# A third score room for the first 34 tiles, q's blocks by DMA, and new durations in the planner of an attention and mixing kernel

## The chip, the core and the metric

The kernel runs on one core of a Trainium2 chip. A core has five engines that run side by side, each through its own list of instructions in order: TensorE (PE, with its weight loads PEld), VectorE (DVE), ScalarE (ACT), GpSimd (POOL) and SyncE (SP). SP starts DMA transfers here. An instruction waits on semaphores until what it needs is there, and everything behind it on the same engine waits with it. The metric is device time in microseconds (us) of one execution, less is better.

## The reference, cut to what matters

```python
# attention: batch 8, heads 8, seq 576, head_dim 64; q, k, v, tau float32
scores = q @ k.T / sqrt(64)
keep   = scores >= max(scores, axis=-1) - tau
attn   = exp(scores - max) where keep, else 0
attn   = attn / (sum(attn) + 1e-9)
x      = (attn @ v), heads side by side          # [8, 576, 512]
# mixing: d_model 512, a causal convolution of 5 taps along seq for each channel
gate_pre[s] = sum over k of conv_w[k] * x[s + k - 4]
out    = (sigmoid(gate_pre) * (x @ w_val)) @ w_out
```

The two weight matrices and `conv_w` come as float64 and are turned into float32 on the chip.

## The kernel before, in words

The work is cut into 32 *jobs*, one for each batch and pair of heads. A job has nine *score tiles* of 128 query rows against 576 keys: one tile that holds the left-over 64 rows of both heads (the *left-over tile*, made from `kh`, `kl` and the block-diagonal `bdq`), and four tiles for each head (from `KH`, `KL` and `Q`). A float32 factor is split into a high and a low part of type float32r, and their products are summed, hence the names that end in h and l.

The life of one tile, with the lines of the profile: TensorE multiplies it into a *score room* `s` of two PSUM banks (L482). DVE takes the row maximum (L486). ACT forms `e`, the exponential (L492), and the threshold (L494). DVE compares, multiplies and sums (L508), and with that the score room is free again. The sums are inverted (POOL L525, DVE L527), the tile is divided by POOL, DVE or ACT (L538, L536, L534), turned by TensorE into `tp` (L588) and copied by ACT into `T` (L599). When half a job's tiles are turned, TensorE multiplies `T` with `v` into a room `acc` of one bank (L627, L634, called *attending* here), and ACT copies it to `xT` (L642). For each job follow the split of `xT` (ACT L667, POOL L671), the first tap of the convolution on POOL (L676), four taps on DVE (L683) and the gate (L691). After the four jobs of a batch come its *products* on TensorE, 192 matmuls with `w_val` and `w_out` into `acc` (L725), with DVE (L752), ACT (L768, L789) and POOL (L772) between and behind them.

PSUM has eight banks: two score rooms (four banks), two rooms `tp`, and two rooms `acc`, which attending and products share.

The next job's k and q are fetched by SP (L304, L308). POOL scales q (L327), ACT and POOL split both (L312, L316, L320, L324), POOL places four blocks of 64 x 64 into `bdq` (L210, in `place`), and SP copies the parts into `KH`, `KL` and `Q` by DMA (L362, L381). While the first jobs run, the weights are turned from float64 as well: 16 pieces, each with five operations on DVE (L224 to L233), two on POOL (L236, L268) and two on ACT (L222, L265).

No loop sets the order. Each operation is declared with an engine, a due time, a planned cost (how long it holds the engine) and a planned time to its end; `carry_out` then runs through planned time, takes on each engine what can begin first, among those the one with the earliest due time, and emits it. So the planned durations and the number of rooms set the order of every engine. In the plan, POOL's operations and some of DVE's (class `DVEp`) exclude each other.

## Time and profile before

| | us |
|---|---|
| timed executions | 775.31, 775.84, 782.68 |
| median | 775.84 |
| span of the profiled execution | 776.5 |
| TensorE busy | 719.6 (93%) |
| VectorE busy | 644.3 (83%) |
| ScalarE busy | 647.2 (83%) |
| GpSimd busy | 475.7 (61%) |

The page gives the profiled execution by its span, from the first to the last instruction; it shows no other time of that execution. A share of busy time is an average over stages, so the stages have to be looked at one by one. TensorE's matmuls overlap one another and their ends are modelled: the mean length of one matmul is longer than the time it adds, and a TensorE that is shown busy is not always at its peak.

### The profile page before, as it was taken

Reading aid. Unit: us, or ns where it says so; the run is one execution under the profiler, and the core shown is the slowest. Engines: PE = TensorE matmul, PEld = TensorE weight load, DVE = VectorE, ACT = ScalarE, POOL = GpSimd, SP = SyncE. Lnnn points to the kernel's source line nnn. Section 1 sums busy time; section 2 is a strip of 40 time slices with the busy share of each in tenths; the row PEclk is TensorE's granted clock in tenths of the full one; section 3 lists DMA queues with packets and bytes.
Section 4 is the critical chain, followed back from the end, with each engine's and each line's share of the span. In section 5 each row is a group of like instructions: output and inputs, shape, how many; then the busy total and the mean of one; then the engine's idle time right before and its main releaser. Section 6 shows DMA issues by size and latency. Waiting matters only on the chain.

```text
span 776.5 us, 15682 instructions
## 1 busy us (share of the span) xinstructions
PE 719.6 (93%) x5216; PEld 607.0 (78%) x5216; DVE 644.3 (83%) x1359; ACT 647.2 (83%) x1477; POOL 475.7 (61%) x698
## 2 busy tenths in 40 slices
PE   3788778979999999999999999998999999999997
PEld 3556457867878888888888888887888888978897
DVE  5989998988888887999878887887888888899830
ACT  5898978978998889899889988897898989888832
POOL 4777655847676775677557675765556764745321
PEclk9999989999999999999999999999999999999999
DMA  6666553535464555555465565553555556540001
GB/s 183 172 170 153 151 149 86 151 91 151 124 156 118 125 148 146 141 135 138 111 164 118 129 152 142 143 131 79 152 151 123 126 136 163 144 98 26 32 31 62
DMA packets 51888, 99.03 MB, mean 128 GB/s; under 512 B 9056, under 2 KB 9056, under 8 KB 51808
## 3 DMA queue, kind: packets, MB, share of 16 engines
q1 hardware_dynamic: 51488, 97.47, 49.0%
q8 instruction: 42, 0.69, 0.4%
q10 hardware_dynamic: 320, 0.56, 0.3%
q14 instruction: 38, 0.31, 0.1%
HBM read 35.74 MB, written 9.44 MB: 58 GB/s over the span
## 4 chain that ended last, share of the span: by engine, by line
PE 68%; DVE 15%; DMA 5%; POOL 4%; ACT 4%; issue 2%; SPq 0%; POOLq 0%; ACTq 0%
PE acc L725 20%; PE s L482 17%; PE acc L634 14%; PE tp L588 13%; DVE nm L486 4%; DVE pp L508 4%; PE acc L627 3%; DMA q_r<-qT 3%; DVE pre L683 3%; ACT e L492 1%; POOL pp L538 1%; DVE spare L229 1%; DVE spare_m L231 1%; POOL ql L324 1%; DVE pp L536 1%
## 5 line engine op out<-in xcount | busy, mean ns | idle before, releaser
L486 DVE TENSOR_REDUCE nm<-s 128x1 f32<-128x576 f32 x288 | 214.9, 752 | 46.9 <-PE s L482 43.6
L492 ACT ACTIVATE e<-s,nm 128x576 f32<-128x576 f32 x288 | 215.3, 747 | 29.9 <-DVE nm L486 16.3
L508 DVE SCALAR_TENSOR_TENSOR pp<-s,nm,e 128x576 f32<-128x576 f32 x256 | 206.8, 811 | 19.9 <-ACT nm L494 18.3
L599 ACT COPY T<-tp 128x384 f32<-128x384 f32 x384 | 175.2, 488 | 26.3 <-PE tp L588 24.8
L482 PE MATMUL s<-KH,Q 128*128 128x288 f32 x512 | 163.4, 334 | 34.2 <-DVE pp L508 23.1
L588 PE MATMUL tp<-ident,pp 128*128 128x128 f32 x1152 | 183.3, 280 | 10.8 <-ACT pp L534 3.6
L588 PEld LDWEIGHTS tp<-ident,pp 128*128 128x128 f32 x1152 | 141.2, 143 | 20.9 <-ACT T L599 5.2
L482 PE MATMUL s<-KL,Q 128*128 128x288 f32 x512 | 147.0, 301 | 0.0
L482 PEld LDWEIGHTS s<-KH,Q 128*128 128x128 f32 x512 | 99.9, 195 | 59.6 <-DVE pp L508 32.2
L634 PE MATMUL acc<-T,v 128*64 128x256 f32 (+1 forms) x1024 | 141.2, 419 | 0.0
L538 POOL TENSOR_SCALAR pp<-pp,sums 128x576 f32<-128x576 f32 x124 | 106.9, 867 | 36.1 <-DVE sums L527 32.2
L683 DVE SCALAR_TENSOR_TENSOR pre<-xT,cw,pre 128x576 f32<-128x576 f32 x128 | 118.6, 926 | 8.8 <-POOL pre L676 8.7
L634 PEld LDWEIGHTS acc<-T,v 128*64 128x64 f32 x1024 | 69.1, 139 | 64.9 <-issue 28.0
L482 PEld LDWEIGHTS s<-KL,Q 128*128 128x128 f32 x512 | 99.9, 195 | 0.0
L525 POOL TENSOR_SCALAR sums<-sums 128x2 f32<-128x2 f32 (+1 forms) x160 | 46.9, 293 | 82.5 <-DVE pp L508 66.1
L494 ACT ACTIVATE nm<-nm,less 128x1 f32<-128x1 f32 x288 | 84.8, 294 | 0.0
L725 PE MATMUL acc<-xl,wvh 128*128 128x320 f32 (+1 forms) x256 | 78.3, 306 | 1.0 <-POOL xl L671 1.0
L725 PE MATMUL acc<-xh,wvl 128*128 128x320 f32 (+1 forms) x256 | 79.2, 309 | 0.0
L725 PE MATMUL acc<-gl,woh 128*128 128x320 f32 (+1 forms) x256 | 78.2, 305 | 1.1 <-POOL gl L772 1.1
L725 PE MATMUL acc<-xh,wvh 128*128 128x320 f32 (+1 forms) x256 | 78.6, 307 | 0.1
L725 PE MATMUL acc<-gh,wol 128*128 128x320 f32 (+1 forms) x256 | 78.6, 307 | 0.0
L725 PE MATMUL acc<-gh,woh 128*128 128x320 f32 (+1 forms) x256 | 78.4, 306 | 0.0
(81 smaller groups left out, 1279.8 us busy)
## 6 DMA issues: line engine op xcount, KB each, us to landing
KH<-kh SPq DMA_DIRECT2D x124, 144.0 KB, 2.6
KL<-kl SPq DMA_DIRECT2D x124, 144.0 KB, 3.5
k_r<-kT SPq DMA_DIRECT2D x32, 320.0 KB, 3.8
v<-vs SPq DMA_DIRECT2D x32, 320.0 KB, 2.9
q_r<-qT SPq DMA_DIRECT2D x32, 288.0 KB, 3.9
outT<-o SPq DMA_DIRECT2D x32, 288.0 KB, 2.4
Q<-qh SPq DMA_DIRECT2D x62, 128.0 KB, 2.3
Q<-ql SPq DMA_DIRECT2D x62, 128.0 KB, 2.4
```

What stands on the lines that cost most here:

```text
L482: nc.tensor.matmul(s[:, a, :HS], w, m, start=i == 0, stop=i == len(terms) - 1)
L486: nc.vector.tensor_reduce(self.nm[:, 0:1], self.s[:, :, :HS], axis=AX.XY, op=ALU.max, negate=True)
L492: nc.scalar.activation(self.e, self.s[:, :, :HS], AF.Exp, bias=self.nm[:, 0:1])
L494: nc.scalar.activation(self.nm[:, 1:2], self.nm[:, 0:1], AF.Identity, bias=less, scale=-1.0)
L508: nc.vector.scalar_tensor_tensor(grp.p[:, i * S : (i + 1) * S].rearrange("p (a f) -> p a f", a=2), self.s[:, :, :HS], self.nm[:, 1:2], self.e,
L525: add = op("POOL", k - 4, 0.2, 0.33, lambda: nc.gpsimd.tensor_scalar(sums(), sums(), 1.0, 1e-9, op0=ALU.mult, op1=ALU.add), [self.kept])
L538: nc.gpsimd.tensor_scalar(v, v, ri(i), 0.0, op0=ALU.mult, op1=ALU.add)
L588: nc.tensor.transpose(tp[:, i * P : (i + 1) * P], self.p[:, k0 : k0 + P], ident)
L599: nc.scalar.copy(T[:, c0 : c0 + n, self.off : self.off + P], tp[:, 0 : n * P].rearrange("p (c q) -> p c q", q=P),)
L634: nc.tensor.matmul(acc[hs, :w], t.v[:, c0 : c0 + D], T[:, h * NKC + c, :], start=False, stop=c == NKC - 1, skip_group_check=True,)
L683: nc.vector.scalar_tensor_tensor(cv, t.xT[:, i : i + S], cw[:, g, i : i + 1], cv, op0=ALU.mult, op1=ALU.add)
L725: nc.tensor.matmul(taken[name, e, j][:, :w], wt[:, c, c0 : c0 + P], moving(c, i)[:, hs], start=n == 0, stop=n == NM - 1,)
```

## The change

It has four parts.

- **Rooms.** `ps_3`, a pool of its own with one more score room (`third`, two banks), stands where the two `acc` banks were. Tiles take it in turn with the other two. When it is given back after tile 34 has been taken, the pool is closed, and its two banks become the two rooms `acc`. Until tile 34, attending uses the rooms `tp`. Products can begin only when `acc` exists.
- **q's blocks.** The four 64 x 64 blocks of each job are copied into `bdq` by SP with DMA, not by POOL.
- **Smaller pieces.** POOL's subtractions for `kl`, `ql`, `xl` and `gl` are cut in two by columns (320 + 320 or 320 + 256), and a product's matmul waits for its own half alone.
- **Planned durations.** An issue of a DMA is planned with 0.56 us (before 0.1, or 0.15 for a pair), landings and several other operations a little longer, and the addition to the sums is due 0.9 tiles earlier.

`Job`, `convolve` and `products` are also written so that a job could cover one half only; here every job has both halves, and this changes nothing by itself.

```diff
+    early = ExitStack()
+    ps_3 = early.enter_context(tc.tile_pool(name="ps_3", bufs=1, space=bass.MemoryType.PSUM))
...
+    class ScoreRooms(Rooms):
+        def __init__(self, pool, n, shape, dtype, name):
+            super().__init__(pool, n, shape, dtype, name)
+            self.third = ps_3.tile(shape, dtype, name="third")
+            self.free.append((0.0, self.third))
+            self.taken = 0
...
+        def give(self, room, when):
+            if room is self.third and self.taken >= THIRD_UNTIL:
+                early.close()
+                ps_a = ctx.enter_context(
+                    tc.tile_pool(name="ps_a", bufs=1, space=bass.MemoryType.PSUM)
+                )
+                for i in range(2):
+                    r_acc.give(ps_a.tile([P, 512], F32, name=f"acc{i}"), when)
+            else:
+                super().give(room, when)
...
-    r_acc = Rooms(ps_a, 2, [P, 512], F32, "acc")
+    r_acc = Rooms(None, 0, [P, 512], F32, "acc")
+    r_s = ScoreRooms(ps_s, 2, [P, 2, 512], F32, "s")
...
+    SEND = 0.56
+    def act(n):
+        return 0.1 + 0.00083 * n
+    def pool1(n):
+        return 0.13 + 0.00102 * n
+    def pool2(n):
+        return 0.17 + 0.00212 * n
+    def tapped(n):
+        return 0.068 + 0.00114 * n
...
-            got_q = op("SP", due - 6, 0.1, 3.8, fetch_q, takes=[r_qr])
+            got_q = op("SP", due - 6, SEND, 4.2, fetch_q, takes=[r_qr])
...
-            self.low_k = op("POOL", due + 1, 1.52, 1.62, low_k, [self.high_k], [r_kl],
-                            [(r_kr, lambda: self.k_r)])
+            for x in (0, SK // 2):
+                self.low_k = [op(
+                    "POOL", due + 1, pool2(SK // 2), pool2(SK // 2) + 0.1, low_k(x, x + SK // 2),
+                    self.low_k, [] if x else [r_kl], [(r_kr, lambda: self.k_r)] if x else [],
+                )]
...
-                        spread(self.bd[hs, which, hs], src[hs, 0:SL].bitcast(F32))
+                        nc.sync.dma_start(
+                            self.bd[hs, which, hs].bitcast(F32), src[hs, 0:SL].bitcast(F32)
+                        )
...
-            self.blocks = [op("POOL", due + 3, 0.45, 0.6, place(0), [high], [r_bd])]
-            self.blocks.append(op("POOL", due + 3, 0.45, 0.6, place(1), [low, self.blocks[0]]))
+            if 0 in self.js:
+                self.blocks = [op("SP", due + 3, 2 * SEND, 2.9, place(0), [high], [r_bd])]
+                self.blocks.append(op("SP", due + 3, 2 * SEND, 2.9, place(1), [low, self.blocks[0]]))
...
-                o = op("SP", due + 1, 0.15, 2.9, copies(name, rooms, src, 0), [done], [rooms])
+                o = op("SP", due + 1, 2 * SEND + 0.1, 3.7, copies(name, rooms, src, 0), done, [rooms])
...
-            add = op("POOL", k - 4, 0.2, 0.33, lambda: nc.gpsimd.tensor_scalar(
+            add = op("POOL", k - 4.9, 0.28, 0.38, lambda: nc.gpsimd.tensor_scalar(
...
-            others = {"DVEp": (0.375, 0.47), "ACT": (0.6, 0.72)}
+            others = {"DVEp": (0.43, 0.52), "ACT": (0.66, 0.78)}
...
+            rooms = r_tp if k < THIRD_UNTIL else r_acc
...
-            cost = 5 * w / 600 + 0.19
+            cost = 5 * w / 600 + 0.27
...
-                    after = [need[c][i], weights[name, c, c0 // CW * CW], *last]
+                    after = [*need[c][j][i], weights[name, c, c0 // CW * CW], *last]
```

What the planner makes of it is seen in the lists of the engines. First TensorE at the start of the program, from the second score tile on. `s0` and `s1` are the score rooms, `KH0` and `Q0` the first job's parts, `tp` the rooms of the transposes and `bdq0` the block-diagonal q; one matmul of each tile stands for its four. Before:

```order
L482 MATMUL s1_102<-KH0_117,Q0_115 128x288
...
L482 MATMUL s0_101<-KH0_117,Q0_115 128x288
...
L482 MATMUL s1_102<-KH0_117,Q0_115 128x288
...
L588 MATMUL tp0_103<-ident_96,pp2_131 128x128 x3
L588 MATMUL tp1_104<-ident_96,pp2_131 128x128 x3
L482 MATMUL s0_101<-kh0_109,bdq0_121 128x288 x2
```

And with the change:

```order
L556 MATMUL s1_104<-KH0_116,Q0_114 128x288
...
L556 MATMUL third_105<-KH0_116,Q0_114 128x288
...
L556 MATMUL s0_103<-KH0_116,Q0_114 128x288
...
L656 MATMUL tp0_101<-ident_96,pp2_130 128x128 x3
L656 MATMUL tp1_102<-ident_96,pp2_130 128x128 x3
L656 MATMUL tp0_101<-ident_96,pp2_130 128x128 x3
L656 MATMUL tp1_102<-ident_96,pp0_128 128x128 x3
L556 MATMUL s1_104<-kh0_108,bdq0_120 128x288 x2
```

The third tile goes into `third`, so it no longer waits until the first tile's room is free. In all, 11 of the 288 tiles go there.

Next SP in the middle of the program, from the copies of one job's Q to those of the next. `KH1`, `KL1` and `Q1` are one job's copies, `k_r0` and `q_r0` the raw k and q of the job after it, `v` its values. Before:

```order
L381 DMA Q1_116<-qh0_111 64x512 x2
L381 DMA Q1_116<-ql0_112 64x512 x2
L362 DMA KH1_118<-kh0_109 64x576 x2
L362 DMA KL1_120<-kl0_110 64x576 x2
L304 DMA k_r0_107<-kT 128x640
L362 DMA KH1_118<-kh0_109 64x576 x2
L362 DMA KL1_120<-kl0_110 64x576 x2
L308 DMA q_r0_108<-qT 128x576
L290 DMA v1_114<-vs 128x640
L381 DMA Q0_115<-qh0_111 64x512 x2
```

And with the change:

```order
L461 DMA Q1_115<-qh0_110 64x512 x2
L461 DMA Q1_115<-ql0_111 64x512 x2
L440 DMA KH1_117<-kh0_108 64x576 x2
L418 DMA bdq0_120<-qh0_110 64x64 x2
L440 DMA KH1_117<-kh0_108 64x576 x2
L440 DMA KL1_119<-kl0_109 64x576 x2
L354 DMA k_r0_106<-kT 128x640
L358 DMA q_r0_107<-qT 128x576
L418 DMA bdq0_120<-ql0_111 64x64 x2
L440 DMA KL1_119<-kl0_109 64x576 x2
L339 DMA v1_113<-vs 128x640
L461 DMA Q0_114<-qh0_110 64x512 x2
```

Two pairs of small DMAs for the next job's blocks now stand among the copies, and the fetch of q stands ahead of the last pair of copies and no longer behind it.

Last, POOL at the end of the program, the low parts `gl` of the last batch. Before:

```order
L671 TENSOR_TENSOR xl1_149<-xT1_141,xh1_143 128x576
L772 TENSOR_TENSOR gl0_162<-g0_156,gh0_158 128x576
L772 TENSOR_TENSOR gl1_163<-g1_157,gh1_159 128x576
L772 TENSOR_TENSOR gl2_164<-g0_156,gh2_160 128x576
L772 TENSOR_TENSOR gl3_165<-g1_157,gh3_161 128x576
```

And with the change:

```order
L862 TENSOR_TENSOR gl1_162<-g1_156,gh1_158 128x320
L862 TENSOR_TENSOR gl1_162<-g1_156,gh1_158 128x256
L862 TENSOR_TENSOR gl2_163<-g0_155,gh2_159 128x320
L862 TENSOR_TENSOR gl2_163<-g0_155,gh2_159 128x256
L862 TENSOR_TENSOR gl3_164<-g1_156,gh3_160 128x320
L862 TENSOR_TENSOR gl3_164<-g1_156,gh3_160 128x256
```

Each low part is two operations, and the first matmuls of the last products need the first of them alone.

## Rows read from the trace of the kernel before

**Rows 1.** The page: busy us of each engine, share of the span, instructions.

```profile
PE 719.6 (93%) x5216; PEld 607.0 (78%) x5216; DVE 644.3 (83%) x1359; ACT 647.2 (83%) x1477; POOL 475.7 (61%) x698
```

**Rows 2.** Busy us by stretch: length, PE, PEld, DVE, ACT, POOL, clock, DMA, GB/s.

```profile
8.00:100.00 92.00, 69.81 (x416) 52.43 (x417) 81.81 (x188) 78.05 (x181) 63.34 (x103) 0.96 0.63 168
100.00:181.00 81.00, 69.27 (x444) 54.74 (x445) 73.77 (x154) 63.88 (x146) 52.16 (x73) 0.89 0.43 112
181.00:500.00 319.00, 314.95 (x2377) 270.38 (x2374) 274.67 (x577) 285.26 (x654) 213.65 (x310) 1.00 0.56 141
500.00:550.00 50.00, 46.35 (x338) 39.36 (x338) 40.62 (x84) 41.54 (x95) 29.96 (x47) 0.97 0.46 113
550.00:743.00 193.00, 190.36 (x1437) 162.34 (x1435) 163.76 (x344) 166.44 (x383) 107.42 (x151) 1.00 0.43 110
```

**Rows 3.** Waits from 8 to 100 us: who waited for whom, total, times, longest.

```profile
DVE nm L486 <- PE s L482: 6.2, 13, 1.4
...
DVE pp L508 <- ACT nm L494: 2.4, 6, 0.7
```

**Rows 4.** Waits from 100 to 181 us.

```profile
DVE nm L486 <- PE s L482: 6.2, 7, 2.6
...
PE acc L627 <- DVE g L752: 2.9, 1, 2.9
```

**Rows 5.** Groups of DVE from 8 to 181 us: count, busy us, mean ns.

```profile
L486 DVE TENSOR_REDUCE nm<-s 128x1 f32<-128x576 f32 x62 | 46.2, 752 | 13.0 <-PE s L482 12.4
...
L683 DVE SCALAR_TENSOR_TENSOR pre<-xT,cw,pre 128x576 f32<-128x576 f32 x20 | 17.4, 872 | 0.0
L231 DVE TENSOR_SCALAR spare_m<-spare 128x256 int32<-128x256 int32 x16 | 10.1, 633 | 0.0
...
L229 DVE SCALAR_TENSOR_TENSOR spare<-woh,spare 128x256 f32<-128x256 f32 x8 | 8.3, 1039 | 0.0
```

**Rows 6.** Single lines over the whole span: shortest, median, longest ns.

```profile
L683 DVE SCALAR_TENSOR_TENSOR pre<-xT,cw,pre x128: 791/811/2090, 53.0 to 749.7; 128x576 f32<-128x576 f32 x128
...
L231 DVE TENSOR_SCALAR spare_m<-spare x16: 276/310/1632, 28.4 to 178.5; 128x256 int32<-128x256 int32 x16
...
L229 DVE SCALAR_TENSOR_TENSOR spare<-woh,spare x8: 414/1122/1637, 100.9 to 177.4; 128x256 f32<-128x256 f32 x8
```

**Rows 7.** Groups of POOL over the whole span.

```profile
L316 POOL TENSOR_TENSOR kl<-k_r,kh 128x640 fp32r<-128x640 f32 x32 | 51.2, 1600 | 14.3 <-ACT kh L312 13.3
...
L772 POOL TENSOR_TENSOR gl<-g,gh 128x576 fp32r<-128x576 f32 x32 | 46.8, 1464 | 19.9 <-ACT gh L768 19.3
...
L210 POOL TENSOR_SCALAR bdq<-ql 64x64 fp32r<-64x64 f32 x64 | 16.6, 259 | 3.8
```

**Rows 8.** SP from 500 to 550 us in order of time: start, us.

```profile
516.25 1.62 SPq L362 DMA_DIRECT2D KH<-kh  x2
517.92 1.23 SPq L362 DMA_DIRECT2D KL<-kl  x2
519.25 0.54 SPq L308 DMA_DIRECT2D q_r<-qT  x1
```

**Rows 9.** The chain that ended last, in the same stretch: start, us.

```profile
519.25 4.54 DMA q_r<-qT
...
525.87 2.62 DVE pp L536 x2
```

**Rows 10.** The copies of Q by SP: issue ns, and us from issue to landing.

```profile
L381 SPq DMA_DIRECT2D Q<-qh x62: 461/467/1259, 24.8 to 689.0; - x62
...
DMA to landing us min/median/max: 2.2/2.4/4.9
```

**Rows 11.** Waits from 740 to 777 us.

```profile
PE acc L725 <- POOL gl L772: 1.1, 1, 1.1
```

**Rows 12.** The tile bdq from 280 to 400 us: ns, first and last start.

```profile
L482 PE MATMUL s<-kh,bdq x20: 290/295/398, 295.2 to 382.0; 128*128 128x288 f32 x20
L210 POOL TENSOR_SCALAR bdq<-ql x12: 234/240/243, 280.1 to 387.5; 64x64 fp32r<-64x64 f32 x12
```

More of the change, by code (lines that the diff above doesn't have):

```diff
@@ L19 @@
 P = 128
-AHEAD = False
-TH = "ACT"
 DIVIDE = ("DVEp", "ACT")
@@ new lines, in low_q, with run @@
+            def low_q(x, y):
+                def run():
+                    if x == a:
+                        self.ql = r_ql.take()
+                    nc.gpsimd.tensor_sub(
+                        self.ql[:, x:y], self.q_r[:, x:y], self.qh[:, x:y].bitcast(F32)
+                    )
+                return run
+            def scale_q():
+                q = self.q_r[:, a:z]
+                nc.gpsimd.tensor_scalar(q, q, sc, 0.0, op0=ALU.mult, op1=ALU.add)
+            got_k = op("SP", due - 6, SEND, 4.2, fetch_k, takes=[r_kr])
@@ L338, in place @@
+            high = op("ACT", due + 1, act(w), act(w) + 0.18, high_q, [scaled], [r_qh])
+            cuts = [a, z] if len(self.js) == 1 else [a, HALVES[0].stop, z]
+            low = [high]
+            for x, y in zip(cuts, cuts[1:]):
+                low = [op(
+                    "POOL", due + 2, pool2(y - x), pool2(y - x) + 0.1, low_q(x, y), low,
+                    [r_ql] if x == a else [], [(r_qr, lambda: self.q_r)] if y == z else [],
+                )]
+            low = low[0]
             def place(which):
@@ L689, in gate, with products @@
         def gate():
-            cv = batch.pre[:, g, :]
+            cv = batch.pre[:, g, a:z]
             nc.scalar.activation(cv, cv, AF.Tanh, scale=0.5)
-        first = op("ACT", k, 0.565, 0.76, high, [t.got_x], [r_xh])
-        part_ = op("POOL", k + 1, 1.4, 1.5, low, [first], [r_xl])
-        last = op("POOL", k, 0.73, 0.8, tap0, [t.got_x, conv_ready, *batch.started],
-                  [r_pre] if g == 0 else [])
-        if g == 0:
+        first = op("ACT", k, act(n), act(n) + 0.19, high, [pair.got_x], [r_xh] if a == 0 else [])
+        last = op("POOL", k, pool1(n), pool1(n) + 0.08, tap0, [pair.got_x, conv_ready, *batch.started],
+                  [r_pre] if g == 0 and a == 0 else [])
+        lows, done = [], [first]
+        for j in js:
+            c = HALVES[j]
+            m = c.stop - c.start
+            done = [op("POOL", k + 1, pool2(m), pool2(m) + 0.1, low(c), done, [] if j else [r_xl])]
+            lows += done
+            batch.made[g][j] = ([first], done)
+        if g == 0 and a == 0:
             batch.started = [last]
         for i in range(1, KT):
-            last = op("DVEp", k + 0.6 * i, 0.74, 0.85, tap(i), [last])
-        free = op("SP", k, 0.0, 0.0, lambda: None, [last, part_], gives=[(r_xT, lambda: t.xT)])
-        batch.made[g] = [first, part_]
-        batch.gate[g] = op("ACT", k + 3, 0.59, 0.76, gate, [last])
-    def products(batch, k, last):
+            last = op("DVEp", k + 0.6 * i, tapped(n), tapped(n) + 0.11, tap(i), [last])
+        if z == S:
+            op("SP", k, 0.0, 0.0, lambda: None, [last, *lows], gives=[(r_xT, lambda: pair.xT)])
+        made = op("ACT", k + 3, act(n), act(n) + 0.17, gate, [last])
+        for j in js:
+            batch.gate[g][j] = made
+    def products(batch, k, last, js):
         b = batch.b
+        a, z = HALVES[js[0]].start, HALVES[js[-1]].stop
+        n_all = z - a
         gs, g, o = {}, {}, {}
@@ L829, in tile_thresholded_attention_gated_mix @@
     batches = [Batch(b) for b in range(B)]
-    for b in range(B):
-        for g in range(NP):
-            if b or g:
-                jobs.append(Job(len(jobs), b, g, len(jobs) * TILES))
+    at = 0
+    for b, g, js in units:
+        if at:
+            jobs.append(Job(len(jobs), pairs[b, g], js, at))
+        at += sum(5 if j == 0 else 4 for j in js)
     tiles = []
@@ L836, in tile_thresholded_attention_gated_mix @@
     for t in jobs:
-        batch = batches[t.b]
-        if t.g == 0:
-            batch.started = []
-        for j in range(2):
+        batch = batches[t.pair.b]
+        for j in t.js:
             half = Half(t, j)
@@ L852, in tile_thresholded_attention_gated_mix @@
             half.attended(len(tiles) - 1)
-        convolve(t, batch, len(tiles))
-        if t.g == NP - 1:
-            last = products(batch, len(tiles) + 4.0, last)
+        convolve(t.pair, batch, len(tiles), t.js)
+        if t.pair.g == NP - 1:
+            last = products(batch, len(tiles) + 4.0, last, t.js)
     carry_out()
```

221 lines of the change are left out of this document (122 added, 99 removed).

## Prediction, made before the change was run

> **What bounds the kernel now.** I read the page's busy times first, then the stretches, and then, in each stretch, the wait that ends last. The page has TensorE at 719.6 of 776.5 us [rows 1], which by itself says neither where the rest is lost nor that TensorE is the bound everywhere. The stretches say it [rows 2]. From 181 to 743 us TensorE is busy for 314.95 + 46.35 + 190.36 = 551.7 of 562 us; it lacks 10.3 us, 3.65 of them between 500 and 550. There TensorE is the bound, and DVE has room (274.67 of 319 in the first of the three). From 8 to 181 us it is the other way round: TensorE is busy for 69.81 + 69.27 = 139.1 of 173 us, and DVE for 81.81 + 73.77 = 155.6. DVE carries the softmax of every tile and the turning of the weights besides, and by 181 us it has reduced 62 tiles [rows 5]. The order of TensorE, of before and of the change, has behind the 63rd tile the same work left: both have attended six jobs there and issued 120 of the 1536 matmuls of products. So the time is about (when the 63rd tile is reached) + (a rest that TensorE fills to 98%), and what the change can win lies mostly in the first term.
>
> DVE's 17.4 us of idle time in that first stretch have two causes. It waits for scores: 6.2 us up to 100 us, with 2.4 more for the threshold from ACT [rows 3], and 6.2 us from 100 to 181 [rows 4]. The scores are late since TensorE waits for a room that DVE itself has to free, two rooms being all there are. Further, DVE is busy longer than it need be. The last multiplication that turns a piece of `w_out` takes 1039 ns in the mean [rows 5] and 414 at the least [rows 6]: 8 x 0.625 = 5.0 us. The mask takes 633 against 276: 16 x 0.357 = 5.7 us. The taps take 872 against 791: 20 x 0.081 = 1.6 us. Together 12.3 us. The longest tap lasts 2090 ns, 1.3 us over the shortest, which is near the length of one of POOL's subtractions (1.46 to 1.60 us) [rows 7].
>
> **The change, part by part.** *Third room.* While it exists, DVE can have three tiles' scores before it, and the idle time it can remove is that up to 100 us, 6.2 + 2.4 = 8.6 us [rows 3]. Ends: 0, if e's two buffers hold the tiles up instead, and 8.6. I take half, 4.3, because only 11 of the first 34 tiles use the room and ACT, at 78.05 of 92 us [rows 2], is not far from full either. What then comes late next is ACT's exponential. Attending in `tp` costs TensorE nothing that it does not have: it is idle a quarter of that stretch.
>
> *From tile 34 to tile 63* there are two score rooms again, and the idle time of 7.2 us (81 - 73.77) [rows 2] can go only through a better order: 2.9 us of TensorE's waiting there was attending that stood behind the products' room [rows 4]. Ends: 3 worse (a stop of that size of its own) and 6 better; I take 1.0 better.
>
> *Smaller pieces.* Each subtraction of 1.46 to 1.60 us [rows 7] becomes two of about half. From the rows of kl, (1600 ns for 640 columns) and gl (1464 for 576) about 2.1 ns a column remain, so the second start adds some 0.1 to 0.2 us: POOL's 128 subtractions grow by 13 to 26 us in all, and the blocks that leave POOL, 128 of 259 ns [rows 7], give back 33 us. POOL is busy for 115.5 of 173 us in the first stretch and covers both. The path gets what DVE waits less behind POOL: between 0 and half of the 12.3 us. I take 2.5, nearer to 0, since half of POOL's work in this stretch, the divisions and the weights' subtractions, is not cut.
>
> The Trainium skill (SBUF — State Buffer, section "SBUF: two separate sides") says that VectorE and GpSimd share a pair of ports by an exclusive lock, held for the whole instruction, so that the loser waits until the other ends. The trace agrees as far as the 2090 ns of a tap go. By that rule alone, with every wait behind a halved subtraction halved, the sum would be 3.7 us lower.
>
> *More divisions on DVE.* Up to tile 72 its order has 10 instead of 7, and two of the 16 pieces of weights come later than before. Priced by the cheapest near neighbour, a tap's 0.79 us [rows 6], three divisions are at most 2.4 us of DVE time, mostly behind 181 us, where DVE has room. I charge 0.5.
>
> *Planned durations, in the stretch from 181 us on.* In SP's list of before, q's fetch stands behind the copies; each pair of them holds SP for 1.2 to 1.6 us [rows 8] where the plan has 0.15. In one such place q_r was sent at 519.25 us and took 4.54 us, divisions came late, two of DVE took 2.62 us, and TensorE stood [rows 9]. The change plans 0.56 us for an issue and puts the fetch ahead of the last copies. Of the 10.3 us I take 2.0 back; ends: 7 better, and 4 worse if the new order has stops of its own.
>
> *Blocks by DMA.* This adds 128 issues to SP of about 0.47 us, 60 us over the span, and each pair lands some 2.4 us after its issue [rows 10], where POOL needed about 0.5 us for a pair. I cost it at nothing: between 280 and 400 us the first blocks were written at 280.1, and the first left-over tile to use any ran at 295.2 [rows 12], so at least 15 us cover 3 us more. Without that cover it costs 0.47 x 2 + 2.4 - 0.5 = 2.8 us a job.
>
> *The end.* TensorE waited 1.1 us for the last low part [rows 11]; with 320 of 576 columns it is ready about 0.65 us sooner (1.46 x 256/576) [rows 7]. I take 0.5.
>
> **Sum.** 4.3 + 1.0 + 2.5 - 0.5 + 2.0 + 0.5 = 9.8 us better: 776.5 - 9.8 = 766.7 us of span. The median of the runs is 0.66 below that span, so **766.0**. About 1% (7.8 us, to 768.1 or 783.6) is what a measurement of this kernel can tell from no change.
>
> **The rivals.**
>
> *No change to speak of.* DVE in the first stretch is bound by its own work, the third room only moves its waits to ACT's e, and the rest is as full as before. For it: DVE is at 90% there and ACT at 82%, and a list written ahead never fills an engine wholly. Against: the waits for scores are there in the rows. What is left is the end and a little of the order: 776.5 - 0.5 - 1 = 775, less 0.66: 774.
>
> *Slower: SP holds up the left-over tile.* The place is the pair of small DMAs between the two halves of `KH`. SP goes in order: when ACT's high part of q is late, SP stands, and both the copies behind it and the blocks reach TensorE late, which goes in order as well. The price is 2.8 us a job, as above. It decides from (9.8 + 7.8)/2.8, about six of the 31 jobs, on; with ten it gives 766 + 28 = 794, with eight 788. Against: the 15 us of cover. For: SP gets 60 us of issues more, and the rows of before know no block by DMA, of 256 bytes a row. On such rows the Trainium skill (DMA: Bandwidth & Descriptors, section "Specifications") says that transfers under 512 bytes lose the full rate, since they are read, changed and written back. No run here shows it yet; by it the landing would be late, and I let the longest landing seen, 4.9 us [rows 10], stand for that in the rows: 5.3 us a job, still within 15.
>
> *A larger gain.* The wait behind POOL's pieces falls by half (6.2 us in place of 2.5), and DVE never lacks scores before tile 34 (8.6 in place of 4.3): 766.0 - 3.7 - 4.3 = 758. The lock of ports in the page cited above speaks for the first half of it. Against: in the order the weights' operations of DVE still stand among POOL's uncut ones.
>
> **How the numbers follow.** Forecast 0.45, no change 0.28, larger gain 0.16, slower 0.11. The range goes from 755, the larger gain with the order's gain from 100 us on four times as large (3 us more), to 777, no change with the worse end of the second term (774 + 3): outside lie the slower case and some 0.09 of the tails. The likeliest case's own range is 762 to 770, by the third room's two ends. Faster by over 1%: 0.38 of the forecast's 0.45, the 0.16, and 0.03 of the no-change case, 0.57. Within 1%: the other 0.07 and 0.25, 0.32. Slower: 0.11.
>
> **What would show it.** Right: the stretch up to the 62nd maximum ends near 173 us and no longer at 181; DVE's waits for scores up to tile 34 fall from 6.2 to some 2 us; the mean of the mask and of `w_out`'s multiplication falls by a tenth or two; TensorE lacks some 8 us, not 10.3, between there and the end of the last attending. Wrong: the 62nd maximum comes at 180 us or later with DVE as busy as before; or a wait of TensorE on DMA for `bdq`, `KH` or `KL` shows up at all; or the stretch behind tile 63 gets longer, which would mean that the new order has stops that I cannot see in the rows of before.

## The result

The change is faster by 1.6%: a median of 764.46 us (764.02 to 765.44, four executions) against 775.77 (775.31 to 782.68) for the kernel before, a ratio of 0.9839 with a 95% interval of 0.9802 to 0.9876. The forecast of 766.0 was right to 1.5 us. Its terms were not.

One and the same order varies too: in one later session 19 executions of the kernel before took from 770.8 to 783.2 us, the shortest at a mean granted clock of 0.991, the longest at 0.976. A profile is one such execution.

The profiled execution has a span of 762.4 us and a time of its own of 764.22; 1.8 us lie around the span here, and 1.7 to 2.1 in the later runs.

### The profile after

The page's busy times, to be read against [rows 1]: each engine does much the same work, in 14 us less.

```profile
PE 715.9 (94%) x5216; PEld 602.5 (79%) x5216; DVE 642.8 (84%) x1365; ACT 643.7 (84%) x1474; POOL 468.0 (61%) x695
```

The same stretches as in [rows 2], with the same columns:

```profile
8.00:100.00 92.00, 70.20 (x423) 52.02 (x423) 81.63 (x190) 79.81 (x184) 58.11 (x89) 0.94 0.64 167
100.00:181.00 81.00, 73.85 (x524) 58.66 (x523) 78.06 (x170) 71.90 (x165) 57.24 (x83) 1.00 0.53 136
181.00:500.00 319.00, 313.45 (x2338) 267.82 (x2337) 274.37 (x576) 278.14 (x644) 207.33 (x304) 0.99 0.55 141
500.00:550.00 50.00, 49.77 (x375) 42.98 (x375) 44.34 (x93) 44.88 (x102) 31.09 (x45) 1.00 0.53 133
550.00:743.00 193.00, 192.97 (x1452) 166.00 (x1453) 161.53 (x333) 161.19 (x370) 109.84 (x162) 1.00 0.43 107
```

The first row has hardly moved. In the second TensorE issues 524 matmuls instead of 444, at a clock of 1.00 instead of 0.89.

Row maxima are the better measure of progress, since there is one for each tile. First DVE's row maxima (L486) before, in two stretches that end at the same tiles, then those of after (L560); the columns are length, DVE's busy time with the count, granted clock, DMA share, GB/s.

```profile
0.00:98.00 98.00, 26.28 (x35) 0.97 0.63 165
98.00:182.00 84.00, 19.93 (x27) 0.90 0.44 116
```

```profile
0.00:97.00 97.00, 25.57 (x36) 0.95 0.65 167
97.00:168.80 71.80, 20.24 (x27) 1.00 0.52 134
```

(The 36th of after begins in the last 0.02 us of the first stretch, and so is counted in both.) From the single maxima in order of time: the 36th began at 98.0 us before and at 97.0 after (1.1 gained, unrounded), the 63rd at 182.2 and 168.8 (12.3 more), and from there to the end it is 594.3 and 593.6 (0.7 more). 27 tiles took 84.1 us and now take 71.9. So **nearly all of the gain lies between tiles 36 and 63**, where the third room no longer exists.

What that stretch looks like, before and then after, with the columns of [rows 2]:

```profile
97.50:181.70 84.20, 71.31 (x457) 56.17 (x456) 76.13 (x161) 66.20 (x152) 53.14 (x74) 0.90 0.44 117
```

```profile
96.50:168.30 71.80, 65.33 (x468) 52.41 (x466) 68.58 (x153) 63.65 (x147) 52.38 (x77) 1.00 0.52 134
```

DVE's idle time falls from 8.1 to 3.2 us and its busy time from 76.1 to 68.6. A part of the busy time is only put off: before, DVE had turned all 16 pieces of the weights by tile 63, and after the change 14 of them. TensorE's clock no longer falls. Three slices of before show when it did:

```profile
110.00:120.00 10.00, 9.54 (x51) 7.29 (x51) 8.79 (x20) 7.61 (x18) 5.70 (x12) 0.69 0.34 93
150.00:160.00 10.00, 6.80 (x52) 6.59 (x52) 10.00 (x20) 6.73 (x16) 7.17 (x10) 1.00 0.62 153
160.00:170.00 10.00, 9.98 (x59) 7.22 (x60) 7.00 (x19) 6.43 (x15) 6.24 (x9) 0.83 0.35 104
```

From 150 to 160 us TensorE stood idle a third of the time behind a full DVE. Right after, it is full at a mean clock of 0.83, and now DVE waits (7.00 of 10). After the change all eight slices from 100 to 180 us are at 1.00.

DVE's waits, up to 100 us and from 100 to 181, against [rows 3, 4]:

```profile
DVE nm L560 <- PE s L556: 7.0, 7, 4.0
...
DVE pp L576 <- ACT nm L567: 0.5, 2, 0.3
```

```profile
DVE pp L576 <- ACT nm L567: 1.3, 4, 0.6
DVE nm L560 <- PE s L556: 0.9, 4, 0.4
```

With three rooms DVE waits for scores in fewer places, 7 and not 13, but for 7.0 us and not 6.2. From 8 us up to tile 34, which begins at 92.3 us before and at 92.1 after, DVE is idle for the same 9.9 us (before, then after, with the columns of [rows 2]):

```profile
8.00:92.30 84.30, 65.65 (x393) 49.47 (x394) 74.39 (x172) 71.87 (x166) 58.58 (x96) 0.96 0.66 175
8.00:92.10 84.10, 64.12 (x381) 46.71 (x381) 74.18 (x173) 71.98 (x164) 51.79 (x79) 0.94 0.64 166
```

From 100 us on there are two rooms again, and the wait for scores falls from 6.2 to 0.9.

DVE's groups from 8 to 181 us, against [rows 5]:

```profile
L763 DVE SCALAR_TENSOR_TENSOR pre<-xT,cw,pre 128x576 f32<-128x576 f32 x24 | 21.5, 894 | 0.0
...
L270 DVE TENSOR_SCALAR spare_m<-spare 128x256 int32<-128x256 int32 x16 | 5.7, 359 | 0.1
...
L268 DVE SCALAR_TENSOR_TENSOR spare<-woh,spare 128x256 f32<-128x256 f32 x8 | 4.8, 598 | 0.0
```

The mask went from 633 to 359 ns, the multiplication from 1039 to 598; the taps, which are the most, did not fall in the mean (872 to 894). Their longest did, from 2090 ns [rows 6] to 1532:

```profile
L763 DVE SCALAR_TENSOR_TENSOR pre<-xT,cw,pre x128: 791/811/1532, 55.3 to 736.6; 128x576 f32<-128x576 f32 x128
```

POOL's pieces, against [rows 7]:

```profile
L368 POOL TENSOR_TENSOR kl<-k_r,kh 128x320 fp32r<-128x320 f32 x64 | 58.8, 923 | 22.4 <-ACT kh L362 21.1
...
L862 POOL TENSOR_TENSOR gl<-g,gh 128x320 fp32r<-128x320 f32 x32 | 29.6, 926 | 22.5 <-ACT gh L855 22.1
...
L862 POOL TENSOR_TENSOR gl<-g,gh 128x256 fp32r<-128x256 f32 x32 | 27.2, 849 | 0.6
```

These two kinds alone grew by 58.8 - 51.2 + 29.6 + 27.2 - 46.8 = 17.6 us; with `ql` (6.5) and `xl` (9.3) it is 33.4 us.

POOL waits less for q's fetch (before, then after, over the span):

```profile
POOL q_r L327 <- DMA q_r<-qT: 35.6, 14, 8.8
POOL q_r L390 <- DMA q_r<-qT: 14.2, 11, 4.6
```

Last, the blocks by DMA (issue ns, then us to landing of both groups on that line, 128 DMAs in all):

```profile
L418 SPq DMA_DIRECT2D bdq<-qh x64: 461/588/1644, 13.7 to 663.6; - x64
...
DMA to landing us min/median/max: 1.7/2.9/7.7
```

### The profile page after: what moved, and what is told of

It reads as the page before. It is cut to its first block, busy times and chain, and to the rows that moved or that the text cites. A ratio compares the mean times of both kernels' runs of the same rounds, so it can differ in the third digit from the quotient of the medians.

```text
span 762.4 us, 15911 instructions
## 1 busy us (share of the span) xinstructions
PE 715.9 (94%) x5216; PEld 602.5 (79%) x5216; DVE 642.8 (84%) x1365; ACT 643.7 (84%) x1474; POOL 468.0 (61%) x695
## 4 chain that ended last, share of the span: by engine, by line
PE 74%; DVE 11%; ACT 7%; DMA 3%; issue 2%; POOL 2%; SPq 0%; POOLq 0%; ACTq 0%; DVEq 0%
PE acc L814 23%; PE s L556 18%; PE tp L656 15%; PE acc L703 14%; PE acc L696 3%; DVE nm L560 3%; DVE pp L576 3%; ACT e L566 2%; DVE pre L763 1%; ACT T L667 1%; DMA q_r<-qT 1%; ACT pp L602 1%; ACT nm L567 1%; DVE spare L265 1%; DVE spare L268 1%
## 5 line engine op out<-in xcount | busy, mean ns | idle before, releaser
L560 DVE TENSOR_REDUCE nm<-s 128x1 f32<-128x576 f32 x277 | 205.9, 752 | 41.5 <-PE s L556 38.5
L566 ACT ACTIVATE e<-s,nm 128x576 f32<-128x576 f32 x277 | 207.4, 749 | 21.2 <-DVE nm L560 11.3
L576 DVE SCALAR_TENSOR_TENSOR pp<-s,nm,e 128x576 f32<-128x576 f32 x245 | 198.0, 811 | 23.4 <-ACT nm L567 22.1
L556 PE MATMUL s<-KH,Q 128*128 128x288 f32 x490 | 153.9, 329 | 21.0 <-DVE pp L576 9.4
L556 PE MATMUL s<-KL,Q 128*128 128x288 f32 x490 | 138.8, 298 | 0.0
L556 PEld LDWEIGHTS s<-KH,Q 128*128 128x128 f32 x490 | 93.9, 192 | 47.0 <-DVE pp L576 15.0
L703 PE MATMUL acc<-T,v 128*64 128x256 f32 (+1 forms) x912 | 123.0, 412 | 0.0
L703 PEld LDWEIGHTS acc<-T,v 128*64 128x64 f32 x912 | 60.4, 136 | 55.5 <-issue 21.9
L593 POOL TENSOR_SCALAR sums<-sums 128x2 f32<-128x2 f32 (+1 forms) x160 | 42.7, 267 | 95.0 <-DVE pp L576 70.9
L556 PEld LDWEIGHTS s<-KL,Q 128*128 128x128 f32 x490 | 94.1, 192 | 0.0
```

Source lines behind the costliest of these rows:

```text
L556: nc.tensor.matmul(s[:, a, :HS], w, m, start=i == 0, stop=i == len(terms) - 1)
L560: nc.vector.tensor_reduce(self.nm[:, 0:1], self.s[:, :, :HS], axis=AX.XY, op=ALU.max, negate=True)
L566: nc.scalar.activation(self.e, self.s[:, :, :HS], AF.Exp, bias=self.nm[:, 0:1])
L576: nc.vector.scalar_tensor_tensor(grp.p[:, i * S : (i + 1) * S].rearrange("p (a f) -> p a f", a=2), self.s[:, :, :HS], self.nm[:, 1:2], self.e,
L593: add = op("POOL", k - 4.9, 0.28, 0.38, lambda: nc.gpsimd.tensor_scalar(sums(), sums(), 1.0, 1e-9, op0=ALU.mult, op1=ALU.add), [self.kept])
L703: nc.tensor.matmul(acc[hs, :w], t.v[:, c0 : c0 + D], T[:, h * NKC + c, :], start=False, stop=c == NKC - 1, skip_group_check=True,)
```

## The experiments

Each is timed against the kernel before, on one chip with it. The medians of the kernel before lie between 775.8 and 778.5 us in these sessions, so runs of different sessions are compared by their ratios to it. Ratios stand with their 95% intervals; "tile 63" is when the 63rd row maximum begins in the profiled execution.

**Two rooms throughout.** The change without its third room.

```diff
-    r_acc = Rooms(None, 0, [P, 512], F32, "acc")
-    r_s = ScoreRooms(ps_s, 2, [P, 2, 512], F32, "s")
+    r_acc = Rooms(ps_3, 2, [P, 512], F32, "acc")
+    r_s = Rooms(ps_s, 2, [P, 2, 512], F32, "s")
-            rooms = r_tp if k < THIRD_UNTIL else r_acc
+            rooms = r_acc
```

> The changed kernel with two score rooms all through; the two banks are the rooms acc from the start, and attending uses them from the start. All else as in the change. Theory A (the planned durations and the pieces carry the gain, the third room is worth about the 1 us by which tile 36 comes earlier): 765 to 767, tile 36 near 98 us, tiles 36 to 63 in about 72 us as with the change. Theory B (the rooms carry it, since the products' rooms that exist only after tile 34 keep early products out of attending's way): 774 to 776, tiles 36 to 63 in 80 us or more with a wait of TensorE's attending on DVE again. Theory C (any new order moves the time by several us either way): anywhere from 760 to 776, with no tie to the wait named.

Measured: 771.43 us, 0.991 [0.9878, 0.9942], tile 36 at 102.0 and tile 63 at 178.1. That is between theories A and B, and within C. By itself this says that the room is worth 0.7% (0.991 against 0.9839), 5.5 us.

**Blocks on POOL.** The change with `bdq` written by POOL as before.

```diff
-                        nc.sync.dma_start(
-                            self.bd[hs, which, hs].bitcast(F32), src[hs, 0:SL].bitcast(F32)
-                        )
+                        spread(self.bd[hs, which, hs], src[hs, 0:SL].bitcast(F32))
-                self.blocks = [op("SP", due + 3, 2 * SEND, 2.9, place(0), [high], [r_bd])]
+                self.blocks = [op("POOL", due + 3, 0.45, 0.6, place(0), [high], [r_bd])]
...
```

> The changed kernel with q's blocks placed by POOL as before, planned with 0.45 us a pair. All else as in the change. If the DMA is free, as costed in the prediction: 764 to 766, POOL busy about 33 us more. If the blocks on POOL took DVE's time through the shared ports: 767 to 770, with longer taps and masks. If SP's 128 issues cost something that the rest hid: 760 to 763.

Measured: 764.63 us, 0.9838 [0.9803, 0.9873]; no difference from the change, as if the DMA were free.

**Whole pieces.** The change with `kl`, `ql`, `xl` and `gl` uncut.

```diff
-            for x in (0, SK // 2):
-                self.low_k = [op(
-                    "POOL", due + 1, pool2(SK // 2), pool2(SK // 2) + 0.1, low_k(x, x + SK // 2),
+            self.low_k = [op(
+                "POOL", due + 1, pool2(SK), pool2(SK) + 0.1, low_k(0, SK),
...
-                    c = HALVES[j]
+                    c = slice(0, S)
...
```

> The changed kernel with POOL's subtractions for kl, ql, xl and gl whole, planned by the same line of 0.17 us + 2.12 ns a column. All else as in the change. If the pieces shorten DVE's waits behind POOL, which is what the prediction took 2.5 us for and the larger rival 6.2: 767 to 771, and the longest tap goes from some 1.7 us up to 2.1 again. If they do not: 763 to 766, with at most 0.5 us at the end.

Measured: 765.63 us, 0.9843 [0.9822, 0.9865]; no difference from the change, as expected if the pieces do not pay. The longest tap is back at 2174 ns:

```profile
L762 DVE SCALAR_TENSOR_TENSOR pre<-xT,cw,pre x128: 791/811/2174, 56.0 to 736.0; 128x576 f32<-128x576 f32 x128
```

**SP's old durations.** The change with the old planned costs and landings of DMAs.

```diff
-    SEND = 0.56
+    SEND = 0.1
-                o = op("SP", due + 1, 2 * SEND + 0.1, 3.7, copies(name, rooms, src, 0), done, [rooms])
+                o = op("SP", due + 1, 0.15, 2.9, copies(name, rooms, src, 0), done, [rooms])
...
```

> The changed kernel with the old planned durations for all DMAs (0.1 us an issue, 0.15 a pair, the old landings), blocks by DMA included. All else as in the change. If SP's planned durations carry the gain: 771 to 776, with POOL's waits for q_r near 36 us again and TensorE's idle time behind tile 63 up by 3 us or more. If they do not: 764 to 767.

Measured: 772.73 us, 0.9936 [0.9915, 0.9958]. Tile 63 comes at 167.1, earlier than in the change; the loss lies behind it. It is the time expected if SP's durations carry the gain, and POOL's wait for q's fetch is back near that of before (35.6), as expected with it:

```profile
POOL q_r L390 <- DMA q_r<-qT: 34.4, 15, 8.5
```

But that wait doesn't set the time by itself: over the span it is 16.2 us in the next experiment, the slowest of all, and 22.1 in the fastest. One wait of TensorE behind tile 63 is the one that the rival of the prediction named:

```profile
PE s L556 <- DMA bdq<-ql: 1.9, 1, 1.9
```

**The third room alone.** The kernel before, with the third room and nothing else.

```diff
-    r_s = Rooms(ps_s, 2, [P, 2, 512], F32, "s")
+    r_s = ScoreRooms(ps_s, 2, [P, 2, 512], F32, "s")
...
+            rooms = r_tp if k < THIRD_UNTIL else r_acc
```

> The kernel before with the third score room until tile 34 alone: old durations, whole subtractions, blocks on POOL. Two rooms in the changed kernel cost some 5 us at tile 36, 9 at tile 63 and about 0.7% of the whole. Theory A (the room is worth that by itself): 0.991 to 0.994 of the time before, tile 36 near 93 us, tile 63 at 172 us or earlier. Theory B (the room pays only where the plan is near the real durations): 0.997 to 1.005, tile 63 at 178 us or later.

Measured: 791.73 us, **1.0183** [1.0139, 1.0228], which neither theory had, although tile 63 comes at 167.1, before the change's 168.8. All is lost behind it. The stretch from 200 to 250 us, and the waits of TensorE over the span:

```profile
200.00:250.00 50.00, 41.89 (x271) 35.36 (x271) 31.75 (x69) 32.30 (x73) 21.65 (x37) 0.83 0.43 114
```

```profile
PE s L508 <- DVE pp L534: 23.3, 19, 3.2
PE tp L614 <- ACT T L625: 9.4, 15, 1.7
```

TensorE is busy 41.89 of 50 us at 0.83, and no other engine is at 65% or over. The last part of `w_out` was turned at 223.4 us (before 184.0, after 182.9): this order had put tiles ahead of weights (by tile 63 DVE had turned 10 of the 16 pieces), and the products behind them came late: by 240 us TensorE had issued 197 of their matmuls, after the change 273.

**The durations alone.** The change's code with two rooms, whole pieces and blocks on POOL, that is the edits of the first three experiments together; against the kernel before only the planned durations and one due time differ.

```diff
-    r_s = ScoreRooms(ps_s, 2, [P, 2, 512], F32, "s")
+    r_s = Rooms(ps_s, 2, [P, 2, 512], F32, "s")
...
+            self.low_k = [op(
+                "POOL", due + 1, pool2(SK), pool2(SK) + 0.1, low_k(0, SK),
...
+                self.blocks = [op("POOL", due + 3, 0.45, 0.6, place(0), [high], [r_bd])]
...
```

> The new planned durations alone: two score rooms, whole subtractions, blocks on POOL, that is, the kernel before with the numbers of the plan changed. Theory A (durations and room each carry a part): 0.990 to 0.994 of the time before. Theory B (the durations are needed only because the blocks went to SP): 0.998 to 1.004.

Measured: 781.44 us, 1.004 [1.0012, 1.0068], tile 63 at 183.9. This is theory B's range; B's reason, the blocks on SP, is not tested by it.

**SP's old durations, blocks on POOL.** The edits of the second and the fourth experiment together.

```diff
-    SEND = 0.56
+    SEND = 0.1
...
-                self.blocks = [op("SP", due + 3, 2 * SEND, 2.9, place(0), [high], [r_bd])]
+                self.blocks = [op("POOL", due + 3, 0.45, 0.6, place(0), [high], [r_bd])]
...
```

> The changed kernel with the old planned durations for DMAs, as in the run that lost some 8 us, but with q's blocks back on POOL. Theory A (the old durations for DMAs hurt by themselves, since SP's order puts q's fetch behind the copies): 0.991 to 0.995, tile 63 to the end 600 us or more. Theory B (they hurt only together with the blocks on SP, 128 issues planned at a sixth of their time): 0.983 to 0.986, tile 63 to the end near 593 us.

Measured: 772.74 us, 0.9938 [0.9911, 0.9966], the same as with blocks by DMA, as theory A has it. Three slices behind tile 63 (at 169.0) show how a loss is made:

```profile
170.00:180.00 10.00, 4.49 (x26) 3.25 (x26) 9.00 (x18) 5.72 (x12) 6.59 (x12) 0.74 0.32 98
180.00:190.00 10.00, 8.28 (x33) 6.87 (x33) 8.06 (x18) 8.44 (x19) 7.51 (x11) 0.50 0.51 117
190.00:200.00 10.00, 10.00 (x66) 6.64 (x64) 6.36 (x16) 7.29 (x18) 8.00 (x15) 0.91 0.70 207
```

```profile
PE s L554 <- POOL bdq L249: 4.3, 2, 4.1
```

TensorE runs dry for 5.5 us, and then, with work again, is granted 0.50, the lower of the two levels (1.2 of 2.4 GHz), so that one stop is counted twice in what TensorE loses: 5.5 us, and then about half of 8.28.

**The other old durations.** The change with the old durations of ACT, DVE, POOL and TensorE, SP's new ones kept.

```diff
-                last = [op("ACT", -20, 1.0, 1.2, lambda h=h: highs(h), last)]
+                last = [op("ACT", -20, 1.3, 1.5, lambda h=h: highs(h), last)]
-            after = [op("ACT", k - DUE[1], 0.81, 1.0, self.weigh, [largest], [r_e])]
+            after = [op("ACT", k - DUE[1], 0.83, 1.0, self.weigh, [largest], [r_e])]
...
```

> The changed kernel with the old planned durations of everything but the DMAs (ACT, POOL, DVE, TensorE, and the old due time of the additions to the sums). Theory A (the planned durations of the engines carry a part): 0.988 to 0.992. Theory B (only those of the DMAs matter): 0.983 to 0.986.

Measured: 769.89 us, 0.9895 [0.9849, 0.9942], tile 63 at 168.7, in theory A's range.

**Third room and durations together**: the change with whole pieces and blocks on POOL, the edits of the second and the third experiment.

```diff
+            self.low_k = [op(
+                "POOL", due + 1, pool2(SK), pool2(SK) + 0.1, low_k(0, SK),
...
+                self.blocks = [op("POOL", due + 3, 0.45, 0.6, place(0), [high], [r_bd])]
...
```

> Third room and new planned durations together, without the other two parts: whole subtractions and q's blocks on POOL. Theory A (these two are all of the gain; alone the room measured 1.018 and the durations 1.004): 0.982 to 0.987 of the time before, TensorE's idle time and lost clock some 8 us less than before up to 170 us and some 8 us less behind it. Theory B (one of the two reliefs of POOL is needed as well, either of them): 0.988 to 0.993, with the lack behind 240 us at 10 us or more, where the runs with one relief have 7 to 8.

Measured: 776.7 us, 1.0001 [0.9963, 1.0039], tile 63 at 174.4. Neither theory had this: the two main parts together give nothing, and yet each of the two small parts could be left out of the change at no cost.

**Five nanoseconds on the change.** One planned duration of the exponential, 5 ns longer; nothing on the chip follows from it but another order.

```diff
-            after = [op("ACT", k - DUE[1], 0.81, 1.0, self.weigh, [largest], [r_e])]
+            after = [op("ACT", k - DUE[1], 0.815, 1.005, self.weigh, [largest], [r_e])]
```

> The changed kernel with 5 ns more in one planned duration, ACT's exponential (0.815 for 0.81 us). Nothing that a plan could be nearer or farther by; but the order of TensorE differs from its 113th row on. Theory A (the gain belongs to the parts): 763 to 767. Theory C (any new order moves the time by several us): 768 or more, or 760 or less, with stops of TensorE between 100 and 240 us that the changed kernel has not.

Measured: **757.29 us** (756.51 to 759.31), 0.9714 [0.9677, 0.975], tile 63 at 166.4. It beats both kernels, and the change by 1.2% of the time before (0.9714 against 0.9839; 7.2 us between medians of two sessions). That is theory C. TensorE, from 240 to 500 and from 500 to 740 us, lacks 0.5 us in all:

```profile
240.00:500.00 260.00, 259.71 (x1964) 222.97 (x1961) 231.75 (x482) 232.35 (x536) 167.92 (x243) 1.00 0.57 142
500.00:740.00 240.00, 239.79 (x1813) 208.21 (x1813) 200.58 (x418) 202.58 (x463) 139.97 (x204) 1.00 0.44 112
```

**The weights planned as long as they take.** The change with DVE's weight operations planned nearer to their means in the trace.

```diff
-        c1, c2 = (0.21, 0.345) if wide else (0.1, 0.12)
+        c1, c2 = (0.29, 0.42) if wide else (0.1, 0.12)
```

> The changed kernel with the weights' operations on DVE planned by what they take in the trace when nothing blocks them: 0.29 us for the mask and the shift (planned 0.21) and 0.42 for the three others (0.345). If durations near the real ones are what saves TensorE's stops where the first products begin: 758 to 763, with less lack between 10 and 240 us (41.8 us with the change). If those stops come from elsewhere: 763 to 767.

Measured: 776.51 us, 0.9968 [0.9937, 0.9999], tile 63 at 173.1, slower than either range. Truer durations did not make a better order here. That is one order, though, with 1.3% between it and the change, and the edit before this one moved the time as far. TensorE waited 3.3 us on blocks once:

```profile
PE s L556 <- DMA bdq<-ql: 3.3, 1, 3.3
```

**Five nanoseconds on the kernel before**, the same edit there.

```diff
-                after = [op("ACT", k - DUE[1], 0.83, 1.0, self.weigh, [largest], [r_e])]
+                after = [op("ACT", k - DUE[1], 0.835, 1.005, self.weigh, [largest], [r_e])]
```

> The kernel before with 5 ns more in the same planned duration, ACT's exponential (0.835 for 0.83 us); TensorE's order differs from its 138th row on. Theory A (an order made by the parts of before gives the time of before, within 1%): 770 to 784, 0.992 to 1.008. Theory C (any new order moves the time by several us, on either side, so that the 1.6% of the change is within what a new order gives by itself): more than 1% from the time before, either way, and the lack of TensorE (idle time and lost clock, 69 us before) changed by as much.

Measured: 786.84 us, 1.0128 [1.0081, 1.0175]. By its time this is theory C. Tile 63 comes at 169.2, as early as in the change, **with two rooms, whole pieces, blocks on POOL and old durations**. From 170 us on it gives all of it back:

```profile
170.00:240.00 70.00, 64.31 (x454) 52.90 (x455) 59.90 (x127) 58.80 (x138) 43.20 (x66) 0.95 0.52 133
240.00:500.00 260.00, 253.34 (x1901) 216.08 (x1902) 224.57 (x469) 226.51 (x521) 162.80 (x238) 1.00 0.54 135
500.00:740.00 240.00, 234.52 (x1758) 200.83 (x1756) 203.52 (x429) 205.21 (x470) 136.40 (x197) 1.00 0.44 112
```

### What the fourteen profiles have in common

In slices of 10 us, TensorE's busy time times its granted clock adds up to 705 to 715 us in every one of them: the work is the same, to within some 5 us either way. The rest of a span is what TensorE *lacks*: idle time, and busy time times (1 - clock). By stretch, in us, sorted by time (3 = third room, N = new durations, H = halves, D = blocks by DMA). The times are medians, the lacks those of the one profiled execution:

| order | parts | time | 0–170 | 170–240 | 240–740 | end | sum |
|---|---|---|---|---|---|---|---|
| change + 5 ns | 3NHD | 757.3 | 40.4 | 5.7 | 0.5 | 4.0 | 50.6 |
| change | 3NHD | 764.5 | 39.6 | 2.1 | 6.5 | 4.0 | 52.3 |
| blocks on POOL | 3NH | 764.6 | 39.7 | 4.0 | 4.1 | 4.1 | 51.9 |
| whole pieces | 3ND | 765.6 | 42.3 | 4.4 | 3.9 | 4.6 | 55.2 |
| other old durations | 3HD, SP's N | 769.9 | 39.4 | 12.1 | 4.1 | 4.2 | 59.8 |
| two rooms | NHD | 771.4 | 46.7 | 3.4 | 2.9 | 4.1 | 57.1 |
| SP's old durations | 3HD, others' N | 772.7 | 39.4 | 7.6 | 3.4 | 4.9 | 55.3 |
| the same, blocks on POOL | 3H, others' N | 772.7 | 41.6 | 13.4 | 2.5 | 4.8 | 62.4 |
| before | – | 775.8 | 48.4 | 5.0 | 10.8 | 5.0 | 69.2 |
| weights planned longer | 3NHD | 776.5 | 42.5 | 13.1 | 4.4 | 4.9 | 64.8 |
| third room, durations | 3N | 776.7 | 44.6 | 9.3 | 4.5 | 5.9 | 64.3 |
| durations alone | N | 781.4 | 53.9 | 4.8 | 6.8 | 6.6 | 72.2 |
| before + 5 ns | – | 786.8 | 40.2 | 8.4 | 12.1 | 8.7 | 69.5 |
| third room alone | 3 | 791.7 | 41.5 | 21.4 | 7.2 | 9.3 | 79.3 |

The lacks explain a difference only where it is larger than those 5 us. Theory C of the last experiment had the lack move with the time; it is 69.5 and was 69.2, and the 4.8 us by which its profiled span is longer stand in the sum of work (711.8 against 707.2).

Three patterns, grouped after seeing them. Up to 170 us the ten orders with the third room lack 39.4 to 44.6 us, the four with two rooms 40.2 to 53.9. From 240 us on, the nine with halves or blocks by DMA lack 0.5 to 6.5 us (and 4.0 to 4.9 at the end), the five with neither 4.5 to 12.1 (and 5.0 to 9.3). In between, from 170 to 240 us, where DVE hands the bound to TensorE, anything from 2.1 to 21.4 is lost, and no part settles it. What goes with it is how long behind tile 63 POOL begins the last low part of `w_out`: in the eight orders where that is less than 25 us, 2.1 to 7.6 are lost, in the six where it is more, 8.4 to 21.4. No run moved the weights and held the rest of the order, so that they are the cause is argued and not shown.

From tile 36 to 63, where nearly all of the change's gain lies, thirteen of the fourteen orders take 68.9 to 76.4 us, whatever their parts, and the kernel before alone takes 84.1. The neutral edit on it takes 71.9, just as the change does.

**What is shown**: the time moves by about 1% with the order alone (1.2% of the time before down on the change, 1.3% up on the kernel before), and no single part carries the gain: without any one of them the ratio is 0.984 to 0.994. **What is open**: how the gain is split over the parts, and how much of it is theirs and not the draw of an order. Taking one away cost nothing to 1.0%, which is what a neutral edit does. Three orders have all four parts (0.971, 0.984 and, with the weights planned longer, 0.997), two have none (1 and 1.013); the three lie below the two, but that is little.

## Why the prediction came out right

- **What bounds the kernel.** Held: in the stretch up to tile 63 DVE is busy for 68.58 of 71.80 us, and from 181 to 743 us TensorE for 556.2 of 562. The 62nd maximum begins at 165.6 us (before 177.8), ahead of the 173 that was to be a sign.
- **The third room, 4.3 us up to tile 34: this step failed.** I let the room remove half of DVE's idle time up to there ("I take half"). Tile 34 comes 0.1 us earlier, DVE's idle time is 9.9 us in both, and the waits for scores stand at 7.0 us in place of 6.2 [rows 3], not some 2. The room does something else. In three pairs of orders that differ by the room alone (two rooms and the change; before and the third room alone; the durations alone and both together) tile 34 comes 5.5, 7.7 and 9.3 us earlier with it, while DVE's idle time changes by +0.2, +1.8 and -1.8: DVE is busy for less, since 1 to 3 fewer of the 16 pieces of weights are turned by then. That work comes later. In the change other parts used the lead up; the new durations alone reach tile 34 13.7 us later than before.
- **The order from tile 34 to 63, 1.0 us: mis-sized.** From tile 36 it is 12.3 us, beyond the upper end of 6. Some 5 are DVE's idle time and 7.5 its busy time, of which the mask and the multiplication of the weights give 9 us (two masks and one multiplication of 8 went behind tile 63) and other operations take some back. I had tied how long DVE's operations last to the length of POOL's pieces, not to the order of both lists, and had left out the clock, 0.90 to 1.00 there. Whether the clock gave time or only followed the order isn't shown; no run holds the one fixed. Nor is it shown that the change's parts gave it: the neutral edit on the kernel before gains as much there with none of them.
- **Smaller pieces, 2.5 us: not shown.** With whole pieces the time is the same within the intervals. The means of the mask and the multiplication did fall, and by more than the tenth or two forecast, but they fall with whole pieces too, in the order of the neutral edit on the kernel before: 488 and 678 ns against 633 and 1039 [rows 5]. POOL's own price was put at 13 to 26 us for all four kinds; it was 33.4. The rows had said so: at 2.1 ns a column, the 1600 ns for 640 columns leave some 0.25 us for a start [rows 7], not 0.1 to 0.2. The price hid, as forecast.
- **The longest tap** goes with the length of POOL's pieces: 2061 to 2174 ns in the six orders with whole pieces, 1426 to 1532 in the eight with halves. The Trainium skill (SBUF — State Buffer, section "SBUF: two separate sides") says that of VectorE and GpSimd the loser waits for the shared ports until the other's instruction ends; the longest tap agrees. The further 3.7 us that the sum would have gained by that rule did not appear as a difference between halves and whole pieces.
- **Divisions, 0.5 us: too small.** From tile 36 to 63, where DVE is the bound, it divides three times and not once, for 2.0 us in place of 0.5; I had put them mostly behind 181 us.
- **Durations behind 181 us, 2.0 us: 0.7 from tile 63 to the end**, the end's gain included. From 181 to 743 us TensorE's idle time fell more than forecast, from 10.3 to 5.8 us (forecast: some 8), by the rows above: 319 - 313.45 + 50 - 49.77 + 193 - 192.97. But those stretches hold other work in the two runs. From tile 63 to the end (before, then after, with the columns of [rows 2]) TensorE's idle time fell by 3.8 us, from 15.0 to 11.2, and its busy time rose by 3.1:

```profile
182.20:776.50 594.30, 579.35 (x4351) 499.02 (x4349) 486.83 (x1013) 500.99 (x1146) 358.38 (x513) 1.00 0.48 123
168.80:762.40 593.60, 582.45 (x4348) 500.00 (x4345) 493.19 (x1027) 499.71 (x1148) 358.94 (x524) 1.00 0.50 127
```

  Its clock lost about 1.4 us there in both. So the idle time went as forecast and more, and a longer busy time for the same matmuls took most of it back. Why it was longer isn't shown; it is within what the sums of work vary by.
- **Blocks by DMA, nothing: right.** The cover held: TensorE never waited for `bdq`, `KH` or `KL`, and POOL does as well. Its one wait on a DMA was for Q:

```profile
PE s L556 <- DMA Q<-ql: 1.0, 1, 1.0
```

  The longest landing, 7.7 us, was beyond the 4.9 that I had let stand for the worst, and within the 15 of cover. The rival's mechanism is real in five other orders with blocks by DMA, once or twice in each and at most 3.3 us long, not ten times over. With blocks on POOL such a wait comes too, of up to 4.1 us (above).
- **The end, 0.5 us: right.** TensorE waited 0.5 us in place of 1.1 [rows 11]:

```profile
PE acc L814 <- POOL gl L862: 0.5, 1, 0.5
```

- **From span to median.** "The median is 0.66 below that span" set two different executions side by side. With 1.9 us around a span, as in other executions of the kernel before, the profiled one took about 778.4 us, so 2.6 more than the median, and the gain in span, 14.1 us, is larger than the 11.3 between the medians. The sum of 9.8 was too small for the first by 4.3 and came near the second for that reason also.

So the total was right by luck: terms that were too large up to tile 36 and behind tile 63, and far too small in between, add up near the median's gain. How much of the gain is the draw of an order is open: with 5 ns more on one planned duration the time is 757, for which the forecast had the rival of a larger gain, with other causes, and with 5 ns more the kernel before has the gain up to tile 63 without the change.

## What to carry to other kernels

Where planned durations set the order of a program, first time an edit that means nothing (5 ns on one duration): here it moved the time by 1%, and no part of a change that is worth less than that can be priced by taking it out once. Do so on the old kernel as well, before a gain in some stretch is put down to the change: the old order may be the odd one. Account for a span as TensorE's work, its idle time and its lost clock by stretch; a stretch that is reached earlier (the third room alone: 15 us earlier) is worth nothing if the next bound engine runs dry there. With a planner that makes orders so cheaply, timing several and keeping the fastest is a way to gain of its own: 757.29 us here.

## What was not expected of the hardware

- After a stop, TensorE pays again: the slice from 180 to 190 us of the kernel with SP's old durations and blocks on POOL was granted 0.50, behind a slice in which it was idle for 5.5 of 10 us. The kernel before shows the same with 0.83 behind a slice of 6.80 us. It does not follow every pause: after the change TensorE was busy for 7.74 us from 100 to 110, and the slices behind stayed at 1.00.
- A DMA of 64 rows of 256 bytes lands later in the median than one of [rows 10], 2.9 us against 2.4, and much later at the most, 7.7 against 4.9; the soonest is earlier, 1.7 against 2.2. Its issue takes SP 588 ns in the median; the copies of Q before take 467 from `qh` and 588 from `ql`, so the smaller size isn't shown to cost SP more.
